# One run of small matmuls per step, from chunk 4 on, in an mLSTM and MLP kernel

## The chip, the cores and the metric

The kernel runs on one core of a Trainium2 chip. The metric is the device time of one execution in microseconds (us), as the median of several runs. The core's engines work side by side: PE (TensorE, matmuls; its weight loads are shown apart as PEld), DVE (VectorE), ACT (ScalarE), POOL (GpSimd) and SP, which here only issues transfers.

## What is computed

An mLSTM layer (4 batches, 8 heads, 768 tokens, head width 40) whose output goes through an MLP (320 to 2048 to 320):

```python
for t in range(S):
    m_new = np.maximum(f_gate[:, :, t] + m, i_gate[:, :, t])
    f_stab = np.exp(f_gate[:, :, t] + m - m_new)
    i_stab = np.exp(i_gate[:, :, t] - m_new)
    m = m_new
    C = f_stab[:, :, None, None] * C + i_stab[:, :, None, None] * np.einsum('bhd,bhe->bhde', vt, kt)
    n = f_stab[:, :, None] * n + i_stab[:, :, None] * kt
    h_tilde = np.einsum('bhde,bhe->bhd', C, qt)
    nq = np.einsum('bhd,bhd->bh', n, qt)[:, :, None]
    denom = np.maximum(np.abs(nq), 1.0)
    o = 1.0 / (1.0 + np.exp(-o_gate[:, :, t]))
    y[:, :, t] = o * h_tilde / denom
...
x = np.ascontiguousarray(attn_out.transpose(0, 2, 1, 3)).reshape(B * S, H * D)
...
h = x @ w_in
sp = np.maximum(h, 0.0) + np.log1p(np.exp(-np.abs(h)))
g = h * erf(sp)
return (g @ w_out).astype(np.float32)
```

## The kernel before

The 768 tokens are cut into 12 chunks of 64. A **step** is one chunk `c` for one pair of batches `r` (0 or 1), so there are 24 steps, two per chunk. A step has four groups of small matmuls, 16 each, on parts of the array of at most 64 rows and 64 columns; a trace shows each as two records, so a group counts 32:

- *carry* (L519): the queries scaled by the decay, `qe`, times the state that the earlier chunks left;
- *gain* (L524): keys times the weighted values `vg`, what this chunk adds to the state;
- *scores* (L510): keys times queries inside the chunk;
- *heads* (L532 from chunk 3 on, L537 before): the weights `dm` times the values. `dm` is the product of the scores and the decay factors, which DVE makes (L568).

`before(r)` holds carry and gain. From chunk 3 on (`JOIN = 3`) carry, gain and scores are one run of instructions on PE. From chunk 4 on three 128x128 transposes of the step of the chunk before (`turned`, L390) stand ahead of them in the same run. The heads are a run of their own, later, once DVE has made `dm`. Behind the heads DVE makes the denominator (`den`, L599 to L601), divides (L611, L613), gates (L618, L620) and brings the state up to date (L625, L628). The gated result is transposed by PE in the next chunk; ACT and DVE cut it into a high and a low part `xh` and `xl` (L403, L407), and these feed the MLP.

The MLP runs in 48 groups, 4 per chunk: up (L760, four products `h` of five matmuls each from group 16 on), a copy and an add to `hb` (ACT L771, DVE L776), softplus and erf on ACT (L780, L784; each change between them, or to exp, loads a table, L887), a product on DVE (L788), a split (L798 or L800, L804), and down (L828, L829, L826), whose results are copied out by L834 and L840.

PSUM holds six pieces that rotate or stay: `pa` has two slots of two banks each, `h` two of one bank, and two banks hold the MLP's results (`pob`). A step takes **both** `pa` slots: one tile `S` for the scores and the transposes, one tile `ph` for the sums `y` (carry plus heads) and `z` (gain).

The order is not left to a scheduler. `ORDER` lists the numbers of all operations in the sequence in which they are issued; a planner made it, with a cost in us for each operation (0.5 for the heads, 1.96 for the run with the transposes, and so on). Each engine works through its operations in that sequence and waits where an input or a slot is not ready.

Of the kernel before, what the change touches and what calls it, by code (L numbers as in the profile page):

```python
# [17 lines left out]
L = 64  # L18
# [15 lines left out]
class Plan:  # L34
# [137 lines left out]
def tile_mlstm_moe(  # L172
# [244 lines left out]
    def attention(c, prev=None):  # L417
# [93 lines left out]

        def before(r):
            y, z = pv(r), pk(r)
            st = state[r]
            for p in range(NPR if c else 0):
                for d in range(2):
                    for j in range(2):
# [431 lines left out]
```

## Time and profile before

| | |
|---|---|
| median of three runs | 454.5 us (454.19 to 454.68) |
| the profiled execution | 454.01 us, its span 452.3 us |
| PE busy | 439.0 us, 97% of the span |
| DVE, ACT, POOL busy | 79%, 75%, 9% |
| granted PE clock | 0.998 of full speed on average |

The profile is one execution. The span runs from the first instruction to the last, and the 1.7 us around it belong to the time but are not resolved. PE's matmuls overlap: a row shows how long one takes from start to end, while the distance between the starts of two neighbours is what the second costs the engine. So the timelines of PE are read by starts.

### The profile page before, as it was taken

What the parts mean: (1) busy time and instruction counts of PE and PEld (TensorE: products, weight loads), DVE (VectorE), ACT (ScalarE), POOL (GpSimd) and SP (SyncE); (2) the same over time, 40 slices, a digit from 0 to 9 for tenths busy, and PEclk for the clock granted to TensorE, in tenths of its full rate; (3) what the DMA queues carried; (4) which work ended last, traced back from release to release, by engine and by line L of the source; (5) the groups of instructions that cost most, each with busy time, mean ns of one, the idle gap of its engine ahead of it and who ended that gap; (6) DMA issues with size and microseconds to landing.
All of it is one profiled execution on the core that took longest, in us unless ns stands there. A gap on an engine that the chain in (4) does not pass through costs nothing.

```text
span 452.3 us, 13080 instructions
## 1 busy us (share of the span) xinstructions
PE 439.0 (97%) x5550; PEld 396.0 (88%) x5550; DVE 355.3 (79%) x710; ACT 338.5 (75%) x532; POOL 38.7 (9%) x62
## 2 busy tenths in 40 slices
PE   6979999999999999999999999999999999999996
PEld 3558988898999999989999998898998999999996
DVE  5899998799878887788969769878798856777471
ACT  4767999898767778978789796758996577783740
POOL 2000051004200102201300030000300000000000
PEclk9999999999999999999999999999999999999999
DMA  7989596847633144413315306132331000001011
GB/s 239 296 246 351 161 333 193 213 114 202 192 95 72 40 141 109 129 58 117 111 51 156 106 20 174 48 109 86 112 120 27 17 16 0 17 0 30 15 30 29
DMA packets 46826, 51.74 MB, mean 114 GB/s; under 512 B 27056, under 2 KB 31664, under 8 KB 46768
## 3 DMA queue, kind: packets, MB, share of 16 engines
q1 hardware_dynamic: 46768, 50.91, 38.6%
q8 instruction: 43, 0.70, 0.6%
q14 instruction: 15, 0.12, 0.1%
HBM read 46.77 MB, written 4.13 MB: 113 GB/s over the span
## 4 chain that ended last, share of the span: by engine, by line
PE 88%; DVE 7%; DMA 2%; issue 1%; ACT 1%; SPq 0%; DVEq 0%; ACTq 0%
PE h L760 39%; PE pob L828 12%; PE pob L826 11%; PE pob L829 11%; PE pa L519 3%; PE pa L532 2%; PE pa L510 2%; PE pob L824 2%; DMA raw<-in_w_in_dram 2%; PE pa L390 2%; PE pa L524 1%; DVE wo L725 1%; PE pa L826 1%; PE pa L829 1%; DMA gt<-in_gates_dram 1%
## 5 line engine op out<-in xcount | busy, mean ns | idle before, releaser
L760 PE MATMUL h<-xh,wh 128*128 128x256 f32 (+1 forms) x768 | 202.1, 343 | 1.0 <-DVE xh L407 0.6
L760 PEld LDWEIGHTS h<-xh,wh 128*128 128x128 f32 x768 | 125.7, 188 | 15.1 <-DVE xh L407 0.8
L760 PE MATMUL h<-xh,wl 128*128 128x256 f32 x384 | 107.9, 281 | 1.0 <-DVE wl L661 1.0
L771 ACT ACTIVATE hb<-h 128x256 f32<-128x256 f32 (+1 forms) x160 | 66.6, 421 | 55.9 <-PE h L760 55.4
L828 PE MATMUL pob<-woh,gh 128*128 128x320 f32 x336 | 101.5, 314 | 0.0
L829 PE MATMUL pob<-wo,gh 128*128 128x320 f32 x336 | 99.9, 309 | 0.0
L776 DVE TENSOR_TENSOR hb<-h,hb 128x256 f32<-128x256 f32 x128 | 53.4, 422 | 44.6 <-ACT hb L771 43.8
L887 ACT ACT_TABLE_LOAD x61 | 78.3, 1283 | 1.9 <-PEq L937 0.8
L760 PEld LDWEIGHTS h<-xh,wl 128*128 128x128 f32 x384 | 72.4, 188 | 2.9 <-DVE wl L661 1.2
L788 DVE TENSOR_TENSOR n<-n,hb 128x1024 f32<-128x1024 f32 x48 | 58.2, 1218 | 9.8 <-ACT n L784 9.8
L829 PEld LDWEIGHTS pob<-wo,gh 128*128 128x128 f32 x336 | 63.1, 188 | 1.7
L828 PEld LDWEIGHTS pob<-woh,gh 128*128 128x128 f32 x336 | 63.2, 188 | 0.9
L826 PE MATMUL pob<-woh,gl 128*128 128x320 f32 x336 | 61.6, 310 | 0.0
L488 POOL TENSOR_SCALAR_AFFINE_SELECT dm<-dm 128x512 f32<-128x512 f32 (+1 forms) x40 | 35.3, 888 | 286.1 <-ACT dm L468 220.0
L804 DVE TENSOR_TENSOR gl<-n,gh 128x1024 fp32r<-128x1024 f32 x45 | 55.4, 1232 | 0.2
L826 PEld LDWEIGHTS pob<-woh,gl 128*128 128x128 f32 x336 | 53.6, 188 | 1.8
L780 ACT ACTIVATE n<-hb 128x1024 f32<-128x1024 f32 x48 | 49.9, 1057 | 1.4 <-DVE hb L776 1.1
L784 ACT ACTIVATE n<-n 128x1024 f32<-128x1024 f32 x48 | 49.9, 1056 | 0.3
L798 ACT ACTIVATE gh<-n 128x1024 fp32r<-128x1024 f32 x29 | 30.3, 1055 | 2.3 <-DVE n L788 2.3
L834 ACT ACTIVATE o<-pob 128x320 f32<-128x320 f32 x22 | 9.6, 435 | 19.9 <-PE pob L826 19.7
L628 DVE TENSOR_TENSOR state<-state,pa 40x328 f32<-40x328 f32 (+1 forms) x36 | 17.8, 494 | 7.4 <-PE pa L532 5.9
L568 DVE TENSOR_TENSOR dm<-pa,dm 128x512 f32<-128x512 f32 x24 | 16.5, 686 | 4.2 <-PE pa L510 3.9
(103 smaller groups left out, 479.6 us busy)
## 6 DMA issues: line engine op xcount, KB each, us to landing
qk<-in_qk_dram SPq DMA_DIRECT2D x24, 512.0 KB
kvo<-in_kvo_dram SPq DMA_DIRECT2D x24, 484.0 KB
eT<-gd SPq DMA_DIRECT2D x44, 128.0 KB
raw<-in_w_out_dram SPq DMA_DIRECT2D x16, 320.0 KB
dm<-gd SPq DMA_DIRECT2D x40, 128.0 KB
raw<-in_w_in_dram SPq DMA_DIRECT2D x8, 512.0 KB
out_dram<-o SPq DMA_DIRECT2D x48, 80.0 KB
raw<-in_w_in_dram SPq DMA_DIRECT2D x4, 256.0 KB
```

What stands on the lines that cost most here:

```text
L488: nc.gpsimd.affine_select(out=x, in_=x, pattern=[[0, H], [1, L]], compare_op=ALU.is_ge, fill=0.0, base=base, channel_multiplier=-1)
L760: nc.tensor.matmul(h[:, n * T:n * T + n_], w, m, start=(s == 0), stop=(s == len(ops) - 1))
L771: nc.scalar.activation(part(), G(f'h{i}')[:, T:2 * T] if wide else G(f'h{i}'), AF.Copy)
L776: nc.vector.tensor_tensor(part(), G(f'h{i}')[:, 0:T], part(), op=ALU.add)
L780: nc.scalar.activation(new('n0', [128, 1024], ('n0', g)), G('hb'), AF.Softplus)
L784: nc.scalar.activation(G('n0'), G('n0'), AF.Erf)
L788: nc.vector.tensor_tensor(G('n0'), G('n0'), G('hb'), op=ALU.mult)
L804: nc.vector.tensor_tensor(new('gl', [128, 1024], ('gl', g), F32R), G('n0'), G('gh').bitcast(F32), op=ALU.subtract)
L826: nc.tensor.matmul(acc(b), G('gl')[:, ts], woh[:, j], start=False, stop=(j == NFF - 1))
L828: nc.tensor.matmul(acc(b), G('gh')[:, ts], woh[:, j], start=(j == 0), stop=False)
L829: nc.tensor.matmul(acc(b), G('gh')[:, ts], t['wol', j], start=False, stop=False)
L887: plan.run(ORDER, lambda k: nc.scalar.preload_act_table_set(KIND[k]), stay)
```

## The change

From chunk 4 on (`LATE = 4`) a step has one PSUM tile, `S`, and one run of small matmuls. The run of step (c, r) is: its own carry and scores, then the heads and the gain of the step that came before it, (c, 0) for (c, 1) and (c-1, 1) for (c, 0). The first run, of step (4, 0), has carry and scores alone, and the heads of the very last step, (11, 1), stay a run of their own (`rest`). So the heads and the gain come half a chunk later than the scores, and the denominator, the division, the gating and the state's update of a step move behind the next step's run.

In the tile, `y` lies behind the scores in its bank, and `z` is written over the scores, which DVE has read by then. The banks of `z` are also dealt out otherwise (`d ^ j` in place of `d`). The three transposes become an operation of their own, `turn`, and write into the same tile once `y` and `z` have been read; the six of chunk 3 are done at once (`turn_both`). All matmuls of the program stay, in number and shape. `ORDER` is made anew from about the 100th us of the program on; the operations before that keep their places on PE.

```diff
-PLAIN, JOIN, GH_ACT, WIDE_UP = (0, 1, 2), 3, 32, 16
+PLAIN, JOIN, LATE, GH_ACT, WIDE_UP = (0, 1, 2), 3, 4, 32, 16
...
+        joint, late = c >= JOIN, c >= LATE
+        home = 'S' if late else 'ph'
...
+        aty, atz = (256, 0) if late else (0, NPR * V1)
+        pv = lambda r, c=c: side(A(home, r, c))[:, :, aty:aty + NPR * V1].rearrange("p j (n d) -> p j n d", d=V1)
+        pk = lambda r, c=c: side(A(home, r, c))[:, :, atz:atz + NPR * V1].rearrange("p d (n e) -> p d n e", e=V1)
...
-                        nc.tensor.matmul(x[sides[d], j, p * L:(p + 1) * L], k, q, start=True, stop=True)
-
-        def before(r):
+                        nc.tensor.matmul(x[sides[d], j, p * L:(p + 1) * L], k, q, start=not late, stop=True, skip_group_check=late)
+
+        def carry(r):
...
+        def gain(r, c=c):
+            z = pk(r, c)
+            for p in range(0 if c == NC - 1 else NPR):
                 for j in range(2):
                     for d, ds in enumerate(sides):
                         h, n = 2 * p + j, D if j or joint else 64
-                        nc.tensor.matmul(z[64 * j:64 * j + n, d, p], A('kvo', r)[ds, h * D:h * D + n], A('vg', r)[ds, h],
-                                         start=(c == 0 and p == 0), stop=False)
...
+                        nc.tensor.matmul(z[64 * j:64 * j + n, d ^ j if late else d, p], A('kvo', r, c)[ds, h * D:h * D + n],
+                                         A('vg', r, c)[ds, h], start=(late or c == 0) and p == 0, stop=late, skip_group_check=late)
...
+        def turn(r, c):
+            plan.part = f'a{c}{r}'
+
+            @op('PE', 0.42, mm=3, r=turned_from(c, r) + [K('S', r, 'y', c)] + ([] if c == NC - 1 else [('st', r)]),
+                w=[K('S', r, 'p', c)], kind='m', tile_=[('xh', ('xh', c)), ('xl', ('xl', c))] * (r == 0))
+            def _():
+                if r == 0:
+                    room(c)
+                turned(c, r, t['S', c, r][:, 0:3 * W])
...
+            step = ((c, 0) if r else (c - 1, 1)) if late and (r or c > LATE) else ()
...
-                if joint:
+                if joint and not late:
                     new('pa', [128, 1024], ('ph', c, r))
                 if was:
                     turned(*was, A('S', r)[:, 256:256 + 3 * W])
                 if joint:
-                    before(r)
+                    carry(r)
+                    if not late:
+                        gain(r)
                 scores(r)
+                if step:
+                    heads(step[1], step[0])
+                    gain(step[1], step[0])
...
+                if step:
+                    after(step[1], step[0])
+                    turn(step[1], step[0])
```

What the new order looks like on the engines is seen best at single steps. PE before, at the run of a step of chunk 6 (`pa` tiles carry numbers here: 2835 is `S`, 2836 is `ph`; `L390` is the step of the chunk before, its result `kvo` transposed):

```order
L829 MATMUL pob0_76<-wo_1758,gh_2438 128x320
L390 MATMUL pa_2835<-ident_65,kvo_1890 128x128 x3
L519 MATMUL pa_2836<-state0_71,qe_2782 64x41 x16
L524 MATMUL pa_2836<-vg_2694,kvo_1744 40x41 x16
L510 MATMUL pa_2835<-qk_2700 64x64 x16
L760 MATMUL h_2892<-xh_2048,wh_73 128x512
```

PE before, at the separate heads of a step of chunk 4:

```order
L829 MATMUL pob0_76<-wo_1817,gh_1931 128x320
L532 MATMUL pa_1983<-kvo_1858,dm_1559 64x41 x16
L826 MATMUL pob0_76<-woh_75,gl_1955 128x320 x4
L828 MATMUL pob0_76<-woh_75,gh_1953 128x320
L829 MATMUL pob0_76<-wo_1742,gh_1953 128x320
```

The first piece has carry, gain and scores behind the transposes; the second is a run of 16 small matmuls between large ones.

PE of the changed kernel, at a run of chunk 6 (2736 is the tile of the step itself, 2483 that of the step before; L520, L512, L537 and L529 are carry, scores, heads and gain, and L831, L899 and L900 are up and down):

```order
L900 MATMUL pob0_76<-wo_1875,gh_2410 128x320
L520 MATMUL pa_2736<-state0_71,qe_2645 64x41 x16
L512 MATMUL pa_2736<-qk_2609 64x64 x16
L537 MATMUL pa_2483<-kvo_1764,dm_1580 64x41 x16
L529 MATMUL pa_2483<-vg_2661,kvo_1764 40x41 x16
L831 MATMUL h_2803<-xh_2243,wh_73 128x512
```

All four groups now stand in one row, and two tiles of two steps are written in it.

ACT of the changed kernel, where the first `xh` of chunk 4 is made from the transposes (L403), and what stands right ahead of it and behind it (L869 is the copy `gh`, L842 the copy `hb`, L958 a table load):

```order
L855 ACTIVATE n0_2025<-n0_2025 128x1024
L958 ACT_TABLE_LOAD
L470 ACTIVATE dm_1927<-dm_1927 128x512
L869 ACTIVATE gh_2251<-n0_1970 128x1024
L842 ACTIVATE hb_2147<-h_2218 128x512
L403 ACTIVATE xh_2243<-pa_1977 128x3x128
L958 ACT_TABLE_LOAD
```

The tile 1977 is free for the next run only when this `xh` and the `xl` behind it on DVE are done. ACT has 58 table loads in the changed kernel, 61 before.

## Rows read from the trace of the kernel before

**Rows 1.** The page's head and first part: busy us, share of the span, instructions.
```profile
span 452.3 us, 13080 instructions
PE 439.0 (97%) x5550; PEld 396.0 (88%) x5550; DVE 355.3 (79%) x710; ACT 338.5 (75%) x532; POOL 38.7 (9%) x62
PEclk9999999999999999999999999999999999999999
```

**Rows 2.** Stretches: each engine's busy us (instructions), granted clock, DMA share, GB/s.
```profile
core 0: us, PE busy (x) PEld busy (x) DVE busy (x) ACT busy (x) POOL busy (x), PEclk, DMA share, GB/s
100.00:125.00 25.00, 24.38 (x271) 22.24 (x270) 23.28 (x49) 20.64 (x34) 8.01 (x8) 1.00 0.65 186
...
125.00:390.00 265.00, 265.00 (x3305) 242.31 (x3304) 210.17 (x424) 205.31 (x311) 19.89 (x24) 1.00 0.28 82
390.00:448.30 58.30, 58.27 (x373) 55.61 (x371) 36.70 (x50) 31.45 (x45) 0.00 (x0) 1.00 0.09 20
```

**Rows 3.** PE's timeline at a step of chunk 4: start us, us, instruction, count.
```profile
119.58 0.41 PE L760 MATMUL h<-xh,wh 128*128 128x256 f32 x2
119.83 0.49 PE L390 MATMUL pa<-ident,kvo 128*128 128x128 f32 x3
120.25 0.68 PE L519 MATMUL pa<-state,qe 40*64 40x41 f32 x32
120.73 0.50 PE L524 MATMUL pa<-vg,kvo 64*40 64x41 f32 x32
121.05 0.68 PE L510 MATMUL pa<-qk 40*64 40x64 f32 x32
121.65 0.41 PE L828 MATMUL pob<-woh,gh 128*128 128x320 f32 x1
121.90 0.31 PE L829 MATMUL pob<-wo,gh 128*128 128x320 f32 x1
122.05 0.31 PE L828 MATMUL pob<-woh,gh 128*128 128x320 f32 x1
...
122.79 0.31 PE L829 MATMUL pob<-wo,gh 128*128 128x320 f32 x1
123.03 0.68 PE L532 MATMUL pa<-kvo,dm 64*64 64x41 f32 x32
123.63 0.85 PE L826 MATMUL pob<-woh,gl 128*128 128x320 f32 x4
124.33 0.31 PE L828 MATMUL pob<-woh,gh 128*128 128x320 f32 x1
```

**Rows 4.** PE's timeline at three transposes that stand alone, near the end.
```profile
377.51 0.40 PE L760 MATMUL h<-xh,wh 128*128 128x512 f32 x1
377.75 0.49 PE L390 MATMUL pa<-ident,kvo 128*128 128x128 f32 x3
377.99 0.39 PE L828 MATMUL pob<-woh,gh 128*128 128x320 f32 x1
378.23 0.31 PE L829 MATMUL pob<-wo,gh 128*128 128x320 f32 x1
378.37 0.31 PE L828 MATMUL pob<-woh,gh 128*128 128x320 f32 x1
```

**Rows 5.** PE's weight loads by shape, 125 to 390 us: busy us, mean ns, idle before.
```profile
L510 PEld LDWEIGHTS pa<-qk 40*64 40x64 f32 x480 | 8.6, 134 | 0.0
L519 PEld LDWEIGHTS pa<-state,qe 40*64 40x64 f32 x480 | 8.4, 134 | 2.5 <-issue 2.0 <-DVE hb L776 0.3 <-DVE dm L464 0.2
L532 PEld LDWEIGHTS pa<-kvo,dm 64*64 64x64 f32 x480 | 8.4, 134 | 3.2 <-issue 2.7 <-DVE hb L776 0.2
L524 PEld LDWEIGHTS pa<-vg,kvo 64*40 64x40 f32 x416 | 5.3, 114 | 0.0
```

**Rows 6.** PE's timeline where it waits for split weights, about 104 and 108 us.
```profile
103.60 0.55 PE L828 MATMUL pa<-woh,gh 128*128 128x320 f32 x1
103.99 0.31 PE L829 MATMUL pa<-wo,gh 128*128 128x320 f32 x1
...
107.36 0.30 PE L828 MATMUL pa<-woh,gh 128*128 128x320 f32 x1
108.28 0.42 PE L829 MATMUL pa<-wo,gh 128*128 128x320 f32 x1 [0.62 <-DVE wo L725]
```

**Rows 7.** DVE's timeline behind a step's heads (which start on PE at 187.91).
```profile
188.66 1.00 DVE L628 TENSOR_TENSOR state<-state,pa 40x328 f32<-40x328 f32 x2 [0.64 <-PE pa L532]
...
190.37 0.17 DVE L599 TENSOR_SCALAR den<-pa 128x8 f32<-128x8 f32 x1
...
191.35 0.66 DVE L613 TENSOR_TENSOR kvo<-pa,den 64x160 f32<-64x160 f32 x2
```

**Rows 8.** PE's timeline at the run that follows them.
```profile
191.55 0.75 PE L826 MATMUL pob<-woh,gl 128*128 128x320 f32 x4
192.15 0.49 PE L390 MATMUL pa<-ident,kvo 128*128 128x128 f32 x3
```

**Rows 9.** ACT's and DVE's timelines behind the lone transposes of 377.75 us.
```profile
378.35 1.28 ACT L887 ACT_TABLE_LOAD   x1
379.64 1.06 ACT L784 ACTIVATE n<-n 128x1024 f32<-128x1024 f32 x1
380.61 0.47 ACT L403 ACTIVATE xh<-pa 128x384 fp32r<-128x384 f32 x1
...
381.11 0.56 DVE L407 TENSOR_TENSOR xh<-pa,xh 128x384 fp32r<-128x384 f32 x1 [1.19 <-ACT xh L403]
```

More of the change, by code (lines that the diff above doesn't have):

```diff
@@ L499, in _ @@
                                             A('dm', r)[:, :, L - 1:L].to_broadcast([128, H, V1]), op=ALU.mult)
-        ends = lambda x: x.rearrange("p (i w) -> p i w", i=4)[:, 0:4:3]
+        ends = lambda x: side(x)[:, :, 0:256] if late else x.rearrange("p (i w) -> p i w", i=4)[:, 0:4:3]
         def scores(r):
@@ L509, in scores @@
                         q, k = (A('qk', r)[js, d, i, p] for i in range(2))
-                        nc.tensor.matmul(x[sides[d], j, p * L:(p + 1) * L], k, q, start=True, stop=True)
-        def before(r):
-            y, z = pv(r), pk(r)
-            st = state[r]
+                        nc.tensor.matmul(x[sides[d], j, p * L:(p + 1) * L], k, q, start=not late, stop=True, skip_group_check=late)
+        def carry(r):
+            y, st = pv(r), state[r]
             for p in range(NPR if c else 0):
@@ L518, in before @@
                         js = slice(64 * j, 64 * j + D)
-                        nc.tensor.matmul(y[lies(d, j), j, p], A('qe', r)[js, d, p], st[js, d, p], start=(p == 0), stop=False)
-            for p in range(0 if last else NPR):
+                        nc.tensor.matmul(y[lies(d, j), j, p], A('qe', r)[js, d, p], st[js, d, p], start=(p == 0), stop=False,
+                                         skip_group_check=late)
+        def gain(r, c=c):
+            z = pk(r, c)
+            for p in range(0 if c == NC - 1 else NPR):
                 for j in range(2):
@@ L531, in heads @@
                     for d, ds in enumerate(sides):
-                        nc.tensor.matmul(y[lies(d, j), j, p], w[ds, j, p], v[ds, 2 * p + j], start=False, stop=(p == NPR - 1))
+                        nc.tensor.matmul(y[lies(d, j), j, p], w[ds, j, p], v[ds, 2 * p + j], start=False, stop=(p == NPR - 1),
+                                         skip_group_check=late)
             for p in range(0 if joint else NPR):
@@ L537, in heads, with weigh @@
                         nc.tensor.matmul(y[os, j, p], w[ds, j, p, ts], v[ds, 2 * p + j], start=False, stop=(p == NPR - 1))
-        early = dict(r=lambda r: ([('st', r), K('qe', r)] if c else []) + ([] if last else [K('vg', r), K('kvo', r, 'k')]),
-                     cost=(0.49 if c else 0) + (0 if last else 0.41), mm=(32 if c else 0) + (0 if last else 32))
+        def weigh(r):
+            plan.part = f'a{c}{r}'
+            @op('DVE', 0.6, r=[K('S', r)], w=[K('dm', r)])
+            def _():
+                x = ends(A('S', r)).rearrange("p j (n t) -> p j n t", t=L)
+                nc.vector.tensor_tensor(dm(r), x, dm(r), op=ALU.mult)
@@ new lines, in after, with _ @@
+        def after(r, c=c):
+            plan.part = f'a{c}{r}'
+            st = state[r]
+            ph = K(home, r, 'y' if late else 0, c)
+            if c == 0:
+                @op('ACT', 0.34, r=[ph], w=[('st', r)])
+                def _():
+                    nc.scalar.activation(st[0:CR], pk(r)[0:CR], AF.Copy)
+            @op('DVE', 0.52, r=[ph], w=[K('den', r, 0, c)], tile_=('den', ('den', c, r)))
+            def _():
+                den = new('den', [128, 2, NPR], ('den', c, r))
+                nq = pv(r, c)[:, :, :, D]
+                nc.vector.tensor_scalar(out=den, in0=nq, scalar1=1.0, scalar2=2.0, op0=ALU.max, op1=ALU.mult)
+                nc.vector.scalar_tensor_tensor(out=den, in0=nq, scalar=-2.0, in1=den, op0=ALU.mult, op1=ALU.max)
+                nc.vector.reciprocal(den, den)
+            by_head = lambda x: x.rearrange("p (n j d) -> p j n d", j=2, d=D)
+            @op('DVE', 0.75 if joint else 0.41, r=[ph, K('den', r, 0, c)], w=[K('kvo', r, 'k', c)])
+            def _():
+                y, z, den = by_head(A('kvo', r, c)[:, 0:DM]), pv(r, c)[:, :, :, 0:D], A('den', r, c).unsqueeze(3)
+                if not joint:
+                    nc.vector.tensor_tensor(y, z, den.to_broadcast([128, 2, NPR, D]), op=ALU.mult)
+                    return
+                nc.vector.tensor_tensor(y[:, 0], z[:, 0], den[:, 0].to_broadcast([128, NPR, D]), op=ALU.mult)
+                for to, at in (sides, sides[::-1]):
+                    nc.vector.tensor_tensor(y[to, 1], z[at, 1], den[at, 1].to_broadcast([64, NPR, D]), op=ALU.mult)
+            @op('DVE', 0.63 if c >= JOIN else 0.43, r=[K('kvo', r, 'k', c)], w=[K('kvo', r, 'o', c)])
+            def _():
+                y = th(r, c)
+                nc.vector.scalar_tensor_tensor(out=y, in0=y, scalar=1.0, in1=A('kvo', r, c)[:, 0:DM], op0=ALU.add, op1=ALU.mult)
+                if c >= JOIN:
+                    nc.vector.tensor_copy(A('kvo', r, c)[:, KV + 320:KV + 384], A('kvo', r, c)[:, KV + 256:KV + 320])
+            if c != NC - 1 and c > 0:
+                @op('DVE', 1.3 if joint else 0.93, r=[K('eT', r, 0, c), ph], w=[('st', r)])
+                def _():
+                    nc.vector.tensor_tensor(st[0:CR], st[0:CR], A('eT', r, c)[0:CR, :, :, L - 1:L].to_broadcast([CR, 2, NPR, V1]),
+                                            op=ALU.mult)
+                    for rows in (slice(0, D), slice(64, CR)) if joint else (slice(0, CR),):
+                        z = pk(r, c)[rows]
+                        nc.vector.tensor_tensor(st[rows], st[rows], z[:, ::-1] if late and rows.start else z, op=ALU.add)
@@ new lines, in turn, with _, turn_both @@
+        def turn(r, c):
+            plan.part = f'a{c}{r}'
+            @op('PE', 0.42, mm=3, r=turned_from(c, r) + [K('S', r, 'y', c)] + ([] if c == NC - 1 else [('st', r)]),
+                w=[K('S', r, 'p', c)], kind='m', tile_=[('xh', ('xh', c)), ('xl', ('xl', c))] * (r == 0))
+            def _():
+                if r == 0:
+                    room(c)
+                turned(c, r, t['S', c, r][:, 0:3 * W])
+        def turn_both(c):
+            plan.part = f'a{c}1'
+            @op('PE', 0.84, mm=6, r=turned_from(c, 0) + turned_from(c, 1), w=[(('p', c), 0)], kind='m', tile_=('pa', ('p', c)))
+            def _():
+                p = new('pa', [128, 1024], ('p', c))
+                for n in range(2):
+                    turned(c, n, p[:, 512 * n:512 * n + 3 * W])
@@ L541, in attention, with room @@
+        def room(c):
+            x = new('xh', [128, 3, 2, T], ('xh', c), F32R)
+            for i, n in enumerate(('xh', 'xl')):
+                t[n, c] = x[:, :, i]
+            t['x', 'both', c] = x
+        early = dict(r=lambda r: ([('st', r), K('qe', r)] if c else []) + ([] if last or late else [K('vg', r), K('kvo', r, 'k')]),
+                     cost=(0.49 if c else 0) + (0 if last or late else 0.41), mm=(32 if c else 0) + (0 if last or late else 32))
         for r in range(2):
             plan.part = f'a{c}{r}'
-            was = (prev, r) if prev is not None else ()
@@ L545, in _ @@
-            @op('PE', 0.64 + (0.42 if was else 0) + (early['cost'] if joint else 0),
-                r=[K('qk', r, n) for n in 'qk'] + ([] if c else [('warm', 0)]) + turned_from(*was) + (early['r'](r) if joint else []),
-                w=[K('S', r)] + ([K('ph', r, 'k')] if joint else []) + ([K('S', r, 'p')] if was else []),
-                tile_=[('pa', ('S', c, r))] + ([('pa', ('ph', c, r))] if joint else []), kind='a',
-                mm=32 + (3 if was else 0) + (early['mm'] if joint else 0), after=[K('dm', r)])
@@ L550, in _ @@
-            def _(r=r, was=was):
+            was = (prev, r) if prev is not None and not late else ()
+            step = ((c, 0) if r else (c - 1, 1)) if late and (r or c > LATE) else ()
+            reads, writes, mm, cost = [], [], 0, 0
+            if step:
+                k, n = step
+                reads = [K('dm', n, 0, k), K('kvo', n, 'v', k)] + ([] if k == NC - 1 else [K('vg', n, 0, k), K('kvo', n, 'k', k)])
+                writes, mm, cost = [K('S', n, 'y', k)], 32 + 32 * (k < NC - 1), 0.5 + 0.41 * (k < NC - 1)
@@ new lines, in _ @@
+            @op('PE', 0.64 + cost + (0.42 if was else 0) + (early['cost'] if joint else 0),
+                r=[K('qk', r, n) for n in 'qk'] + ([] if c else [('warm', 0)]) + turned_from(*was) + (early['r'](r) if joint else []) + reads,
+                w=[K('S', r)] + ([K('ph', r, 'k')] if joint and not late else []) + ([K('S', r, 'p')] if was else []) + writes,
+                tile_=[('pa', ('S', c, r))] + ([('pa', ('ph', c, r))] if joint and not late else []), kind='a',
+                mm=32 + mm + (3 if was else 0) + (early['mm'] if joint else 0), after=[K('dm', r)])
@@ L551, in _ @@
+            def _(r=r, was=was, step=step):
                 new('pa', [128, 1024], ('S', c, r))
-                if joint:
+                if joint and not late:
                     new('pa', [128, 1024], ('ph', c, r))
@@ L556, in _, with rest @@
                 if joint:
-                    before(r)
+                    carry(r)
+                    if not late:
+                        gain(r)
                 scores(r)
+                if step:
+                    heads(step[1], step[0])
+                    gain(step[1], step[0])
+            if late:
+                weigh(r)
+                if step:
+                    after(step[1], step[0])
+                    turn(step[1], step[0])
+                if r == 0:
+                    if c == LATE:
+                        turn_both(prev)
+                    divided(prev, [K('S', n, 'p', prev) if c > LATE else (('p', prev), 0) for n in range(2)])
+        if late:
+            def rest():
+                plan.part = f'a{c}1'
+                @op('PE', 0.5, mm=32, r=[K('dm', 1), K('kvo', 1, 'v')], w=[K('S', 1, 'y')], kind='a')
+                def _():
+                    heads(1)
+                after(1)
+                turn(1, c)
+                divided(c, [K('S', n, 'p') for n in range(2)])
+            return rest
         if prev is not None:
@@ L563, in attention @@
         for r in range(2):
-            plan.part = f'a{c}{r}'
-            @op('DVE', 0.6, r=[K('S', r)], w=[K('dm', r)])
-            def _(r=r):
-                s = ends(A('S', r)).rearrange("p j (n t) -> p j n t", t=L)
-                nc.vector.tensor_tensor(dm(r), s, dm(r), op=ALU.mult)
+            weigh(r)
         for r in range(2):
@@ L578, in _ @@
                     new('pa', [128, 1024], ('ph', c, r))
-                    before(r)
+                    carry(r)
+                    gain(r)
                 if r == 0:
-                    x = new('xh', [128, 3, 2, T], ('xh', c), F32R)
-                    for i, n in enumerate(('xh', 'xl')):
-                        t[n, c] = x[:, :, i]
-                    t['x', 'both', c] = x
+                    room(c)
                 heads(r)
         for r in range(2):
-            plan.part = f'a{c}{r}'
@@ L589, in attention @@
-            st = state[r]
-            if c == 0:
-                @op('ACT', 0.34, r=[K('ph', r)], w=[('st', r)])
-                def _(r=r, st=st):
-                    nc.scalar.activation(st[0:CR], pk(r)[0:CR], AF.Copy)
-            @op('DVE', 0.52, r=[K('ph', r)], w=[K('den', r)], tile_=('den', ('den', c, r)))
-            def _(r=r):
-                den = new('den', [128, 2, NPR], ('den', c, r))
-                nq = pv(r)[:, :, :, D]
-                nc.vector.tensor_scalar(out=den, in0=nq, scalar1=1.0, scalar2=2.0, op0=ALU.max, op1=ALU.mult)
-                nc.vector.scalar_tensor_tensor(out=den, in0=nq, scalar=-2.0, in1=den, op0=ALU.mult, op1=ALU.max)
-                nc.vector.reciprocal(den, den)
@@ L603, in attention @@
-            by_head = lambda x: x.rearrange("p (n j d) -> p j n d", j=2, d=D)
-            @op('DVE', 0.75 if joint else 0.41, r=[K('ph', r), K('den', r)], w=[K('kvo', r, 'k')])
-            def _(r=r):
-                y, z, den = by_head(A('kvo', r)[:, 0:DM]), pv(r)[:, :, :, 0:D], A('den', r).unsqueeze(3)
-                if not joint:
-                    nc.vector.tensor_tensor(y, z, den.to_broadcast([128, 2, NPR, D]), op=ALU.mult)
-                    return
-                nc.vector.tensor_tensor(y[:, 0], z[:, 0], den[:, 0].to_broadcast([128, NPR, D]), op=ALU.mult)
-                for to, at in (sides, sides[::-1]):
-                    nc.vector.tensor_tensor(y[to, 1], z[at, 1], den[at, 1].to_broadcast([64, NPR, D]), op=ALU.mult)
@@ L615, in _ @@
-            @op('DVE', 0.63 if c >= JOIN else 0.43, r=[K('kvo', r, 'k')], w=[K('kvo', r, 'o')])
-            def _(r=r):
-                y = th(r)
-                nc.vector.scalar_tensor_tensor(out=y, in0=y, scalar=1.0, in1=A('kvo', r)[:, 0:DM], op0=ALU.add, op1=ALU.mult)
-                if c >= JOIN:
-                    nc.vector.tensor_copy(A('kvo', r)[:, KV + 320:KV + 384], A('kvo', r)[:, KV + 256:KV + 320])
-            if not last and c > 0:
-                @op('DVE', 1.3 if joint else 0.93, r=[K('eT', r), K('ph', r)], w=[('st', r)])
-                def _(r=r, st=st):
-                    nc.vector.tensor_tensor(st[0:CR], st[0:CR], A('eT', r)[0:CR, :, :, L - 1:L].to_broadcast([CR, 2, NPR, V1]),
-                                            op=ALU.mult)
-                    for rows in (slice(0, D), slice(64, CR)) if joint else (slice(0, CR),):
-                        nc.vector.tensor_tensor(st[rows], st[rows], pk(r)[rows], op=ALU.add)
+            after(r)
@@ L845, in tile_mlstm_moe @@
             gate_block(k)
-        attention(k, prev)
+        rest = attention(k, prev)
         if prev is not None:
@@ L873, in tile_mlstm_moe @@
     if prev is not None:
-        finish(prev)
+        rest()
         for g in range(4 * prev, 4 * prev + 4):
```

17 lines of the change are left out of this document (7 added, 10 removed), and 122 rows, old and new, of the table ORDER.

## The prediction

> **What bounds the kernel now.** I read the page's first part, then the busy times by stretch, then PE's timeline. PE is busy 97% of the span [rows 1]; the reader should look at the stretches behind that mean. From 125 to 390 us PE is busy 265.00 of 265.00 us, and from there to 448.3 us all but 0.03 us; DVE and ACT are busy about 79% and 77% in the long stretch, and the clock is 1.00, the upper level of 2.4 GHz, all the time [rows 2]. So no wait ends last there: the time is the sum of what PE's instructions cost, and only fewer or cheaper instructions, or less lost between them, shorten it. Between 100 and 125 us PE loses a little, and DVE, at 23.28 of 25 us, is nearly as full [rows 2].
>
> PE's timeline then shows what is lost between instructions; it is to be read by starts. Inside a row of large matmuls the next L828 or L829 starts 0.15 us after the last (121.90 to 122.05) [rows 3]. At the border of a run of small ones this spacing breaks three times. **Into** the run: L829 at 122.79, the heads at 123.03, so 0.24, 0.09 too much. **Out** of it: the heads take 0.60 to the next large start, while 32 small ones with the same weight loads (carry, 120.25 to 120.73) take 0.48 when another small group follows: 0.12 more. **Behind** it: 121.65 to 121.90 is 0.25, 0.10 too much, and the four L826 from 123.63 to 124.33 take 0.70 in place of 4 x 0.147, 0.11 too much [rows 3]. A border pair thus costs 0.09 + 0.12 + 0.10 = 0.31 us.
>
> **The change, part by part.** Matmuls and their shapes stay; the runs of small ones fall from 46 in the program to 31, counted in the two orders. The 15 that go are heads: of the 16 steps from chunk 4 on, all but the last give up their own run.
>
> *A step before* [rows 3]: from the transposes at 119.83 to the large matmul at 121.65 is 1.82, plus 0.10 behind, 1.92. Its heads: 0.09 in, 0.60, 0.11 behind, 0.80. Together 2.72 us.
>
> *A step after.* The run: in 0.09; carry 0.48; scores 0.48 to 0.50 (their 0.60 less the way out, 0.11); heads 0.48; gain 0.32 (120.73 to 121.05) plus the way out, 0.45; behind it 0.10. That is 2.10. The transposes now stand alone; their price is shown near the end: 377.75 to 377.99 is 0.24, and the next large start comes 0.24 later in place of 0.15, so 0.33 [rows 4]. In the old run they cost 0.42 (119.83 to 120.25) [rows 3], of which 0.09 is the way in that the new run pays itself, so moving them costs nothing. Together 2.43 us.
>
> The difference is 0.29 a step, and 15 x 0.29 = **4.4 us**, all of it on PE and so on the path that sets the end.
>
> *What isn't shown.* Scores followed by heads, and heads followed by gain, occur nowhere before. Between groups that do follow each other the hand-over is at most 0.04 us (carry's 0.48 to gain against 31 spacings). It could be dearer, since the heads' first matmuls wait for DVE, POOL and transfers. The ends are 0.02 and 0.31 (a full border); I take 0.04, since carry to gain also waits for DVE and a transfer and costs just that. A gain from a dearer hand-over is excluded.
>
> *The late heads.* The denominator, division, gating and state update stay on DVE in number and size (I take the reversed bank order in the state's add as free; both banks are read anyway), and come half a chunk later. Who waits for them: the next run needs the state, and a run's tile is free again only when `xh` and `xl` have read the transposes. Before, the tight place was another: both slots belonged to one step, and the next run waited for DVE to read `ph`. At 188.66 DVE begins with the state, the last division ends at 192.01 [rows 7], and the next run enters at 192.15, without a gap behind the four L826 [rows 8]: 0.1 us to spare. After, state and division have until the transposes and the run after, 5 us and more of PE work. The new tight place is transposes to next run. By the order, five of these distances are short: three times four L826 and ten wide (or sixteen narrow) L831, 2.46 us, then 3.05 and 3.64; the others are over 5 us. `xh` takes 0.47 and `xl` 0.56, together 1.1 us with the hand-over [rows 9]. So 1.4 us are to spare if ACT and DVE come at once; the cover is PE's up and down matmuls.
>
> *ACT* loses three table loads of 1.28 us [rows 9]; off the path, nothing.
>
> *The reshuffled stretch, 100 to 125 us.* PE waits there for DVE's split weights: 0.39 between 103.60 and 103.99 and 0.92 between 107.36 and 108.28, in place of 0.15 each, so 1.0 us [rows 6]. The new order lets sixteen up matmuls ahead of the first of them and spreads the splits, which could save all of it; but DVE has no more room than before. Between 1.0 saved and 2 lost (the longer wait, 0.8, twice, and a bit) I take 0.3 saved, near the present state.
>
> **Sum.** Profiled execution 454.0 - 4.4 - 0.3 = 449.3 us. The median of the runs stands 0.5 above the profiled one, so **449.8 us**.
>
> **The rivals.**
>
> *The hand-over is a border too.* If PE drains between scores and heads because the heads' inputs are waited for there, 0.27 of the 0.29 a step is given back: the change then doesn't do what it says: 15 x 0.27 = 4.1, 453.9. Half of it gives 451.8. For it speaks that an entry shows up to 0.2 us idle of the weight loads ahead of heads under "issue" (2.7 us in 15 heads) [rows 5]; against it that carry to gain and gain to scores, with waits, show nothing of the kind.
>
> *Banks.* Before, gain's two row halves write two banks; with `d ^ j` neighbours of different row halves write one bank. Heads do that already, and need 0.48 to a follower just as carry does, whose row halves write different banks; so the rows give this no price. Gain's lower price goes with its narrower weights, 114 against 134 ns a load [rows 5]. If it were the banks after all, gain would cost what heads cost: 0.16 more in 14 steps, 2.2 us, 452.0. The Trainium skill, "TensorEngine Tiling (Array Packing)", Restrictions and Gotchas, says that different row tiles cannot access the same PSUM bank at once; by that rule 452.0, and the trace of the heads speaks against a price.
>
> *Late `xh`: slower.* ACT works in order. At 377.75 the transposes stand alone, and `xh` begins only at 380.61, behind a table load and an erf; `xl` ends at 381.67, 3.7 us after the transposes' end [rows 4, 9]. Before, no run waited for that. With this delay at all five short places PE would wait 3 x 1.2 + 0.7, 4.3 us: 454.1, no change. One more 1024-wide pass of 1.06 ahead of `xh` makes it 3 x 2.3 + 1.7 + 1.1, 9.7 us: 459.5. It ends slower from a mean wait of 1.2 us at the five places on. Against it: at the places I followed, the order has `hb`, `gh` or `dm`, not a table load, right ahead of `xh`; at one of the five a load stands two places ahead.
>
> *Scattered waits*, 1 to 3 us in all, most likely about 100 to 125 us: 451 to 452.5.
>
> **How the numbers follow.** Forecast 0.66; scattered waits 0.12; dear hand-over 0.08 (half of it within 0.2%); banks 0.05; late `xh` 0.09 (slower, or no change at its edge). The range, 448.2 to 453.2, goes from all of the early waits saved and a cheap hand-over to the rivals that keep a small gain; it leaves the last rival and the full border out, with some of the forecast's own edge. A run can tell 0.2%, 0.9 us, from no change. Faster 0.87, same 0.06, slower 0.07.
>
> **What would show it.** In the changed profile L520, L512, L537 and L529 should follow each other in about 2.0 us, 15 times less a border; L390 alone should show 0.24 and 0.24 again; PE should be as full from 125 us on. The prediction is wrong if heads start more than 0.55 us behind the start of the scores, if gain takes 0.45, or if PE's timeline shows gaps before L520 that end with DVE `xh` L407.

## The result and the profile after

The changed kernel takes **451.09 us** (median of 6 runs, 450.6 to 452.0), the kernel before beside it 454.83: a ratio of 0.991, 95% interval 0.988 to 0.994. So it is faster, as forecast, but by less: 3.7 us (0.9%) in place of 4.7. The time lies inside the range that was given. Its page, to be read against [rows 1]:

```profile
span 450.0 us, 13070 instructions
PE 436.6 (97%) x5550; PEld 395.6 (88%) x5550; DVE 356.8 (79%) x710; ACT 332.7 (74%) x529; POOL 41.1 (9%) x62
```

PE has the same 5550 instructions and lost 2.4 us of busy time; ACT lost three instructions, the table loads. The windows of time, as in [rows 2] (busy us of each engine, granted clock, DMA share, GB/s):

```profile
100.00:125.00 25.00, 23.61 (x234) 20.96 (x233) 24.58 (x47) 22.11 (x38) 4.73 (x6) 1.00 0.62 176
125.00:390.00 265.00, 264.79 (x3390) 244.73 (x3389) 213.07 (x429) 198.47 (x309) 25.52 (x26) 1.00 0.30 86
390.00:446.00 56.00, 55.95 (x359) 53.48 (x357) 35.13 (x47) 32.02 (x45) 0.00 (x0) 1.00 0.07 17
```

From 125 us on PE is as full as before and the clock is at its upper level. Between 100 and 125 us PE idles 1.4 us where it had idled 0.6, and DVE is busy 24.58 of 25. PE's timeline at a run of chunk 5, and at lone transposes (start us, us, instruction, count), answers [rows 3, 4]:

```profile
137.98 0.49 PE L390 MATMUL pa<-ident,kvo 128*128 128x128 f32 x3
138.23 0.83 PE L897 MATMUL pob<-woh,gl 128*128 128x320 f32 x4
...
140.58 0.40 PE L831 MATMUL h<-xh,wh 128*128 128x256 f32 x2
140.91 0.68 PE L520 MATMUL pa<-state,qe 40*64 40x41 f32 x32
141.40 0.67 PE L512 MATMUL pa<-qk 40*64 40x64 f32 x32
141.89 0.63 PE L537 MATMUL pa<-kvo,dm 64*64 64x41 f32 x32
142.33 0.50 PE L529 MATMUL pa<-vg,kvo 64*40 64x41 f32 x32
142.76 0.51 PE L831 MATMUL h<-xh,wh 128*128 128x256 f32 x2
143.11 0.28 PE L831 MATMUL h<-xh,wl 128*128 128x256 f32 x1
```

Here `h<-xh` is up, `woh,gl` is down, and L520, L512, L537 and L529 are carry, scores, heads and gain. The second L831 of the pair at 140.58 starts 0.12 later, so the way in takes 0.21 in place of the usual 0.12: 0.09 too much. Scores follow carry after 0.49, heads follow scores after 0.49, gain follows heads after 0.44: no border inside. The whole run takes 1.85 to the next large start, and the two L831 behind it take 0.35 in place of 0.24. The other runs of the changed kernel that hold all four groups show the same 1.85, but for one of 1.92 at 287.4 us.

**A ruler without the first 100 us.** Up to a row of L895 at about 100 us (L824 in the kernel before) PE's order is the same in both kernels, yet this row starts between 98.8 and 102.8 us in the nine profiled executions of this study. So a single execution carries up to 4 us of chance ahead of the change; in this one PE waited 2.6 us for DVE's `xh` at about 30 us, in the profile of before 0.6. From there the distance to the last four matmuls that read `gl` is steadier: the changed kernel's two executions give 344.73 and 344.62. Before, and after:

```profile
99.43 1.34 PE L824 MATMUL pa<-wo,n 128*128 128x320 f32 x4
...
447.52 0.75 PE L826 MATMUL pob<-woh,gl 128*128 128x320 f32 x4
```

```profile
100.47 1.34 PE L895 MATMUL pa<-wo,n 128*128 128x320 f32 x4
...
445.20 0.75 PE L897 MATMUL pob<-woh,gl 128*128 128x320 f32 x4
```

That is 348.09 and 344.73 us, 3.4 us less; the profiled spans differ by 2.3 only because this execution of the changed kernel came 1.0 late to the first row. I use this distance, called the ruler, beside the medians.

| kernel | median us | ruler: from, to | us |
|---|---|---|---|
| before | 454.8 | 99.43, 447.52 | 348.09 |
| changed | 451.1 | 100.47, 445.20 | 344.73 |
| changed, again (e_after) | 451.8 | 101.13, 445.75 | 344.62 |
| one border a run (e_border) | 458.3 | 102.78, 453.67 | 350.89 |
| same matmul ahead (e_ahead) | 452.4 | 100.51, 447.42 | 346.91 |
| three borders a run (e_three) | 467.2 | 99.06, 460.24 | 361.18 |
| DVE order (e_dve) | 448.8 | 98.82, 441.57 | 342.75 |
| no masks (e_nomask) | 449.8 | 102.70, 444.55 | 341.85 |
| xh three times (e_xh) | 458.0 | 101.01, 452.12 | 351.11 |

**Where the rest went.** PE's waits between 112 and 120 us, with POOL and DVE beside them (the bracket is idle time and who ended it). POOL runs the masks here, affine selects that zero the decay weights of later tokens (L490). On DVE, L585 and L587 gate, L796 splits the down weights, L859 makes the product, and L875 splits it into `gl`:

```profile
111.05 4.93 POOL L490 TENSOR_SCALAR_AFFINE_SELECT dm<-dm 128x512 f32<-128x512 f32 x6 [34.79 <-ACT dm L470]
...
111.34 0.94 DVE L585 SCALAR_TENSOR_TENSOR kvo<-kvo 128x320 f32<-128x320 f32 x1
...
112.31 0.56 DVE L587 COPY kvo<-kvo 128x64 f32<-128x64 f32 x1
...
112.78 2.69 DVE L796 TENSOR_TENSOR wo<-wo,woh 128x320 fp32r<-128x320 f32 x3
112.92 0.14 PEld L390 LDWEIGHTS pa<-ident,kvo 128*128 128x128 f32 x1 [0.36 <-DVE kvo L587]
...
114.67 0.41 PE L900 MATMUL pa<-wo,gh 128*128 128x320 f32 x1
...
115.39 1.66 DVE L859 TENSOR_TENSOR n<-n,hb 128x1024 f32<-128x1024 f32 x1
115.52 0.19 PEld L900 LDWEIGHTS pa<-wo,gh 128*128 128x128 f32 x1 [0.55 <-DVE wo L796]
...
118.36 1.22 DVE L875 TENSOR_TENSOR gl<-n,gh 128x1024 fp32r<-128x1024 f32 x1
...
119.63 1.44 PE L897 MATMUL pa<-woh,gl 128*128 128x320 f32 x8 [0.75 <-DVE gl L875]
```

By starts, against the usual spacing, PE loses 0.28 ahead of the last transposes, 0.26 and 0.46 ahead of two L900 and 0.91 ahead of L897. With 0.24 at 106.9, 0.20 at 121.2, 0.23 at 147.7 and 0.29 at 260.3 that is 2.9 us; the kernel before loses 0.24 and 0.78 [rows 6] and two smaller ones, 1.3 in all. The 0.24 in either sum is no wait for DVE: the profile shows no idle time of PE or its weight loads there, and the second L899 or L900 behind a row of L895 (L824 before) comes that late in all nine traces. It stands on both sides and drops out. So 1.6 us came back, nearly all of it as waits for DVE, and the work itself fell by 3.4 + 1.6 = 5.0 us. Behind a wait the next matmul starts about 0.1 late as well (114.67 to 114.92 is 0.25 in place of 0.15); with that, both figures are about 0.2 larger.

### The profile page after: what moved, and what is told of

Same layout as the page of the kernel before. It is cut to its first block, busy times and chain, and to the rows that moved or that the text cites. A ratio compares the mean times of both kernels' runs of the same rounds, so it can differ in the third digit from the quotient of the medians.

```text
span 450.0 us, 13070 instructions
## 1 busy us (share of the span) xinstructions
PE 436.6 (97%) x5550; PEld 395.6 (88%) x5550; DVE 356.8 (79%) x710; ACT 332.7 (74%) x529; POOL 41.1 (9%) x62
## 4 chain that ended last, share of the span: by engine, by line
PE 86%; ACT 4%; DVE 4%; DMA 3%; issue 1%; POOL 0%; SPq 0%; DVEq 0%; POOLq 0%
PE h L831 37%; PE pob L899 11%; PE pob L900 11%; PE pob L897 11%; PE pa L520 3%; PE pa L512 2%; PE pob L895 2%; PE pa L537 2%; DMA raw<-in_w_in_dram 1%; PE pa L529 1%; PE pa L390 1%; ACT L958 1%; DMA dm<-gd 1%; PE pob L284 1%; PE pa L449 1%
## 5 line engine op out<-in xcount | busy, mean ns | idle before, releaser
L831 PE MATMUL h<-xh,wh 128*128 128x256 f32 (+1 forms) x768 | 206.4, 346 | 2.7 <-DVE xh L407 2.6
L831 PEld LDWEIGHTS h<-xh,wh 128*128 128x128 f32 x768 | 128.1, 190 | 16.6 <-DVE xh L407 2.8
L842 ACT ACTIVATE hb<-h 128x256 f32<-128x256 f32 (+1 forms) x160 | 66.3, 421 | 72.8 <-PE h L831 72.5
L831 PE MATMUL h<-xh,wl 128*128 128x256 f32 x384 | 108.4, 282 | 0.2 <-DVE wl L732 0.2
L899 PE MATMUL pob<-woh,gh 128*128 128x320 f32 x336 | 100.8, 312 | 0.0
L900 PE MATMUL pob<-wo,gh 128*128 128x320 f32 x336 | 99.9, 309 | 0.0
L831 PEld LDWEIGHTS h<-xh,wl 128*128 128x128 f32 x384 | 72.9, 190 | 1.6 <-DVE wl L732 0.4
L859 DVE TENSOR_TENSOR n<-n,hb 128x1024 f32<-128x1024 f32 x48 | 58.8, 1229 | 9.0 <-ACT n L855 8.9
L900 PEld LDWEIGHTS pob<-wo,gh 128*128 128x128 f32 x336 | 63.1, 188 | 1.6
L899 PEld LDWEIGHTS pob<-woh,gh 128*128 128x128 f32 x336 | 63.3, 188 | 0.2
L490 POOL TENSOR_SCALAR_AFFINE_SELECT dm<-dm 128x512 f32<-128x512 f32 (+1 forms) x40 | 37.7, 951 | 277.9 <-ACT dm L470 274.5
L897 PE MATMUL pob<-woh,gl 128*128 128x320 f32 x336 | 62.5, 310 | 0.0
L897 PEld LDWEIGHTS pob<-woh,gl 128*128 128x128 f32 x336 | 54.4, 188 | 2.3
L875 DVE TENSOR_TENSOR gl<-n,gh 128x1024 fp32r<-128x1024 f32 x45 | 54.8, 1227 | 0.3
L869 ACT ACTIVATE gh<-n 128x1024 fp32r<-128x1024 f32 x29 | 30.5, 1056 | 0.0
```

The costliest lines, as they stand in the source:

```text
L490: nc.gpsimd.affine_select(out=x, in_=x, pattern=[[0, H], [1, L]], compare_op=ALU.is_ge, fill=0.0, base=base, channel_multiplier=-1)
L831: nc.tensor.matmul(h[:, n * T:n * T + n_], w, m, start=(s == 0), stop=(s == len(ops) - 1))
L842: nc.scalar.activation(part(), G(f'h{i}')[:, T:2 * T] if wide else G(f'h{i}'), AF.Copy)
L859: nc.vector.tensor_tensor(G('n0'), G('n0'), G('hb'), op=ALU.mult)
L875: nc.vector.tensor_tensor(new('gl', [128, 1024], ('gl', g), F32R), G('n0'), G('gh').bitcast(F32), op=ALU.subtract)
L897: nc.tensor.matmul(acc(b), G('gl')[:, ts], woh[:, j], start=False, stop=(j == NFF - 1))
```

## Experiments

### Is the gain the borders?

e_border puts one matmul into the run of the changed kernel, between scores and heads: a full 128 x 128 weight load, 64 columns, into columns that nobody reads. In e_ahead the same call stands ahead of `carry(r)`. Line numbers of the kernel shift by a few where lines are added:

```diff
+        def wide_one(r):
+            nc.tensor.matmul(A('S', r)[:, 420:484], wh[:, 0, 0:128], wh[:, 0, 128:192], start=False, stop=True, skip_group_check=True)
...
                 scores(r)
                 if step:
+                    wide_one(r)
                     heads(step[1], step[0])
```

> The changed kernel again, unchanged, as the measure for the other runs of this group. Expected 451.1 us. The profiled execution read so far had PE waiting 2.6 us for DVE xh L407 at 29 to 35 us, in a part where both kernels have the same order. If this is the transfers of one execution, another execution shows another figure there (0.6 to 1.6 as in the kernel before), and the waits of PE for DVE between 112 and 120 us (0.28, 0.26, 0.46 and 0.91 us) come back, since they follow from DVE's order; if those are chance too, they are gone or stand elsewhere.

> One matmul of 128 x 64 with a full 128 x 128 weight load, into columns that nobody reads, between the scores and the heads in each of the 15 runs of the changed kernel: the old border comes back and nothing else is moved. Theory (the gain is the borders): 15 times the matmul's own cost (an estimate from 0.12 to 0.14 us a start beside large ones: 2 us) and 15 x 0.27 to 0.32 = 4.1 to 4.9 us of borders, so about 457.2 (456.8 to 458.2). Rival (the gain came from the changed order on DVE and ACT, three table loads and later heads, and a border costs nothing): 453.2, the own cost alone.

> The same 15 matmuls of 128 x 64, but ahead of the carry, next to the large matmuls, so that no border is added. Both theories: 451.1 and 15 times the own cost of 0.12 to 0.14 us, 453.1 (452.6 to 453.5). What tells the theories apart is the difference between the run with the matmul inside and this one: 4.1 to 4.9 us by the border theory, under 0.5 us by the rival.

e_after came to 451.8 us with the same four waits (0.29, 0.25, 0.46, 0.91), so these follow from the order; its early waits were others. e_border came to 458.3 and e_ahead to 452.4: a difference of 5.9 us, by the ruler 4.0. PE's timeline at the same run, first e_border, then e_ahead:

```profile
143.17 0.40 PE L835 MATMUL h<-xh,wh 128*128 128x256 f32 x2
143.50 0.68 PE L523 MATMUL pa<-state,qe 40*64 40x41 f32 x32
143.99 0.67 PE L515 MATMUL pa<-qk 40*64 40x64 f32 x32
144.59 0.30 PE L506 MATMUL pa<-wh 128*128 128x64 f32 x1
144.82 0.68 PE L540 MATMUL pa<-kvo,dm 64*64 64x41 f32 x32
145.31 0.50 PE L532 MATMUL pa<-vg,kvo 64*40 64x41 f32 x32
```

```profile
140.63 0.40 PE L836 MATMUL h<-xh,wh 128*128 128x256 f32 x2
140.87 0.20 PE L506 MATMUL pa<-wh 128*128 128x64 f32 x1
141.00 0.68 PE L523 MATMUL pa<-state,qe 40*64 40x41 f32 x32
141.49 0.67 PE L515 MATMUL pa<-qk 40*64 40x64 f32 x32
```

With the matmul inside, scores to matmul is 0.60, matmul to heads 0.23, heads to gain 0.49: 1.32 in place of 0.49 + 0.44, 0.39 more. Ahead of carry it makes the entry 0.25 in place of 0.21, 0.04 more: its own cost nearly vanishes in the way in that is there anyway, where I had expected 0.12. So a border, priced as the same matmul inside the run against ahead of it, is 0.35 us, and 15 of them are 5.2 us. All 15 runs of e_border show the same 0.34 up to the heads. By the ruler the two differ by less, since each execution has waits of its own. e_ahead has three (0.61 at 182, 0.65 at 184 and 0.52 at 323 us); without them it is 0.5 us longer than e_after, 15 x 0.03. e_border has one of 0.92 at 328 us; without all these the difference is 4.8 us. The rival that the gain came from other changes of the order is out: everything else was left as it was, and the borders alone give back the 5.0 us that the work had lost.

> The narrow-column matmul of the run with one border put not only between scores and heads, but also between carry and scores and between heads and gain: 15 + 15 + 14 of them. The run with one border spent 0.386 us a run more than the changed kernel by its trace (scores to the matmul 0.604, from it to the heads 0.227, heads to gain 0.488, against 0.494 and 0.439). Theory (any switch to a full-size matmul and back costs that, whatever the groups): 44 x 0.386 = 17.0 us over the changed kernel in the part of the trace behind 100 us, a median of 468 us (466 to 470). Rival (the border is dear only ahead of the heads, whose inputs come from DVE, POOL and transfers): 15 x 0.386 + 29 x 0.034 (the matmul's own cost beside large ones) = 6.8 us, 458.

e_three, with the call also between carry and scores and between heads and gain, measured 467.2; by the ruler it is 16.5 us longer than the changed kernel, 44 x 0.375 (0.5 of it is a wait of its own at 330 us). The four groups of a run now start at:

```profile
140.62 0.68 PE L523 MATMUL pa<-state,qe 40*64 40x41 f32 x32
...
141.45 0.69 PE L515 MATMUL pa<-qk 40*64 40x64 f32 x32
...
142.31 0.68 PE L540 MATMUL pa<-kvo,dm 64*64 64x41 f32 x32
...
143.14 0.52 PE L532 MATMUL pa<-vg,kvo 64*40 64x41 f32 x32
```

That is 0.83, 0.86 and 0.83 in place of 0.49, 0.49 and 0.44, so 0.34, 0.37 and 0.39 more. The border is no matter of the heads and their inputs; it costs about the same at all three places.

### Is the give-back DVE's order?

> The changed kernel with five DVE operations moved in the order: the weight splits 12 and 15 (L796) behind the gating of chunk 3 (L585, L587) and the splits 10 and 11; L859 of group 10 and the splits 1 and 2 (L796) behind the second vg (L500) of chunk 4. PE's, POOL's and the transfers' orders stay. Theory (the give-back of 1.6 us is DVE's order between 112 and 120 us): the waits of 0.28, 0.26, 0.46 and 0.91 us go and no others come, so 1.3 to 2.0 us less than the changed kernel in the same group, 449.4. Rival (DVE as a whole is full there, slowed by POOL's masks, and any order only moves the wait): within 0.5 us of the changed kernel, with the same sum of waits at other instructions between 112 and 140 us.

Five numbers of the order table, all of them work of DVE, moved: 273 and 279 behind 271, and 435, 251 and 253 behind 522. **448.8 us** (448.1 to 450.4), 0.987 of the kernel before (0.983 to 0.990): faster than both kernels, and by the ruler 1.9 to 2.0 us shorter than the changed one's two executions. Its DVE and PE about 110 us, and its window from 100 to 125 us:

```profile
108.65 0.48 DVE L585 SCALAR_TENSOR_TENSOR kvo<-kvo 128x320 f32<-128x320 f32 x1
109.17 0.20 DVE L587 COPY kvo<-kvo 128x64 f32<-128x64 f32 x1
109.28 3.95 DVE L796 TENSOR_TENSOR wo<-wo,woh 128x320 fp32r<-128x320 f32 x5
...
110.45 0.82 PE L390 MATMUL pa<-ident,kvo 128*128 128x128 f32 x6
...
113.73 1.21 DVE L875 TENSOR_TENSOR gl<-n,gh 128x1024 fp32r<-128x1024 f32 x1
```

```profile
100.00:125.00 25.00, 24.44 (x226) 23.17 (x225) 23.45 (x45) 23.79 (x37) 5.85 (x6) 1.00 0.60 168
```

The six transposes run through in 0.82 in place of 1.16 us, `gl` begins 14.9 us behind the first row of the ruler in place of 17.9, and the four waits are gone; 0.44 come back ahead of L520, for DVE's `xh`. PE's order is the same instruction for instruction and most of what was lost there is won, so the rival (DVE full, any order only moves the wait) is out. The masks still lengthen the splits here (five L796 take 3.95 us), but PE no longer waits for these.

### Does POOL slow DVE?

e_nomask leaves the masks out from chunk 4 on, and with them a part of the computation:

```diff
-                    for rows, base in ((128, L), (64, 0)):
+                    for rows, base in () if c >= LATE else ((128, L), (64, 0)):
```

> The changed kernel without POOL's masks (affine selects on the decay weights, L490) from chunk 4 on, so that later tokens enter the sum: part of the computation is left out, and nothing is moved. In the changed kernel DVE's instructions are longer while POOL runs from 111.05 to 115.98: L585 0.94 in place of 0.49, L587 0.56 in place of 0.20, three L796 2.69 in place of 1.5, L859 1.66 in place of 1.22, 2.4 us together, and PE's waits of 0.28, 0.26, 0.46 and 0.91 us for DVE stand right there and behind. Theory (POOL's masks slow DVE, and with DVE's order that makes the waits): DVE's instructions fall back to the shorter figures, PE's waits of 1.9 us between 112 and 120 go, and so do the 0.23 at 147.8 and the 0.29 at 260.3: 1.9 to 2.4 us less behind 100 us than the changed kernel, a median near 449.2. Rival (DVE's longer records have another cause, transfers into the same memory for example): the durations and the waits stay, 451.4.

449.8 us, and by the ruler 2.8 to 2.9 us shorter than the changed kernel's two executions. DVE's timeline at the same instructions:

```profile
113.57 0.49 DVE L585 SCALAR_TENSOR_TENSOR kvo<-kvo 128x320 f32<-128x320 f32 x1
114.10 0.20 DVE L587 COPY kvo<-kvo 128x64 f32<-128x64 f32 x1
114.20 1.54 DVE L796 TENSOR_TENSOR wo<-wo,woh 128x320 fp32r<-128x320 f32 x3
115.66 1.22 DVE L859 TENSOR_TENSOR n<-n,hb 128x1024 f32<-128x1024 f32 x1
```

0.94, 0.56, 2.69 and 1.66 fell to 0.49, 0.20, 1.54 and 1.22, and all of PE's waits between 112 and 120 us are gone, those at 147.7 and 260.3 too; ahead of L520 the wait grew by 0.17, for `xh`. The rival with another cause of the long records (transfers) is out: the masks alone were taken away. So two things made the give-back, each shown by its own run: DVE's order, and POOL's masks that lie beside it.

### What late `xh` costs

e_xh makes ACT's copy three times:

```diff
-                nc.scalar.activation(t['xh', c][:, :, ts], pt(), AF.Copy)
+                for _ in range(3 if c >= LATE else 1):
+                    nc.scalar.activation(t['xh', c][:, :, ts], pt(), AF.Copy)
```

> The changed kernel with ACT's copy of the transposes (xh, L403, 0.49 us) made three times instead of once from chunk 4 on: xh and xl come 0.98 us later, everything else stays. It prices the rival that late xh stops the next run. The prediction reckoned 1.4 us to spare at the five short places; then no run waits and the time stays 451.4 (within 0.5). By the changed kernel's trace xl ended 0.14 us ahead of the run at 183.5, 0.83 ahead of that at 336.3, 0.94 at 269.6, 1.16 at 140.9 and 1.29 at 218.6, over 1.8 at the others: then waits of about 0.9, 0.2 and 0.1 us come ahead of L520, 1.2 us, and ACT's 30 us of further work may add as much again elsewhere: 452.6 to 454.

458.0 us, by the ruler 6.4 us longer than the changed kernel: far over both figures. ACT, DVE and PE behind the transposes of 182.16 us:

```profile
182.89 1.53 ACT L404 ACTIVATE xh<-pa 128x384 fp32r<-128x384 f32 x3
...
183.69 0.50 PE L832 MATMUL h<-xh,wh 128*128 128x512 f32 x1 [0.45 <-DVE hb L848]
...
186.21 0.68 PE L521 MATMUL pa<-state,qe 40*64 40x41 f32 x32 [0.39 <-DVE xh L408]
```

Ahead of the runs PE waits longer at three places (154.4, 186.2 and 274.0 us by 0.2, 0.4 and 0.8), about 1.5 us. The sum is near the 1.2 that was expected, the places are only in part: one wait ends with `xh`, the other two with `qe`, which DVE also makes. Most of the rest are waits of 0.1 to 0.9 ahead of L832 (up), for `hb`: ACT is busy 347 us in place of 333 (32 further copies of 0.47, 15 us, not the 30 that I had put down), and the reading of the up matmuls' result stands in the same queue. I had left those out. So the run prices more than late `xh`: it fills ACT's queue as well.

## Why the prediction came out as it did

- **What bounds the kernel** held: from 125 us on PE is full, and less work on PE shortened the time by as much, but for the waits.
- **The borders**: forecast 15 x 0.29 = 4.4, measured 5.0 to 5.2 as work, and 5.2 by putting them back. The joins are free, scores to heads and heads to gain as well as carry to scores. The heads inside the run took 0.44 to the next group in place of the 0.48 that I counted; behind a large matmul (e_border) they take 0.49. So the 0.48 of a group behind a large matmul seems to hold some of the border's cost; no run separates it.
- **The transposes alone**: moving them costs nothing, as forecast. They take 0.25, and some 0.08 more stand behind them (four L897 take 0.67 from 138.23 on, usually 0.59).
- **The reshuffled stretch** is the term that was mis-sized. I took 0.3 us saved, within bounds of 1.0 saved and 2 lost; 1.6 were lost, most of them in 100 to 125 us. I wrote that DVE has no more room than before, and then chose a value near no change. The row of DVE at 23.28 of 25 us [rows 2] spoke for the upper bound: the new order brought the gating of chunk 3, its splits and the next chunk's masks closer together, and POOL's masks lengthen just those instructions of DVE. The wait behind the 0.92 in [rows 6] looks like the same thing already: four L725 took 3.29 us there, from 105.46 on, beside masks that ran from 103.06 to 107.89, and seven of them 2.90 us from 100.19 on, beside none. I read it as order alone; no run took the masks out of the kernel before. The 0.39 of [rows 6] I read as a wait too, and it is none (see above); so at most 0.8 could have been saved.

```profile
100.19 2.90 DVE L725 TENSOR_TENSOR wo<-wo,woh 128x320 fp32r<-128x320 f32 x7
...
103.06 4.83 POOL L488 TENSOR_SCALAR_AFFINE_SELECT dm<-dm 128x512 f32<-128x512 f32 x4 [27.84 <-ACT dm L468]
...
105.46 3.29 DVE L725 TENSOR_TENSOR wo<-wo,woh 128x320 fp32r<-128x320 f32 x4
```

- **The median**: 454.5 - 5.0 + 1.6 = 451.1, the measured time; that it fits to a tenth is chance, since from the 454.83 measured beside it the sum is 451.4. By its number it is the case "scattered waits", 451 to 452.5, which I gave 0.12; the forecast's mechanism was right and one term mis-sized by 1.9 us, of which the borders gave 0.6 back.
- **Dear hand-over** is out: the joins show no border, and where one was put, 5.2 us came.
- **Banks** is out: gain takes 0.43 to the next large start, way out included, where 0.45 was reckoned without a price for the banks, and its weight loads take 116 ns in place of 114 [rows 5]. The Trainium skill, "TensorEngine Tiling (Array Packing)", Restrictions and Gotchas, says that different row tiles cannot access the same PSUM bank at once; these rows show no price of that.
- **Late `xh`** did not cost anything here, but by luck. At 183.5 us `xl` ended 0.14 us ahead of the run, where I had reckoned 1.4: DVE came to it 1 us after ACT was done. The run's weight loads already stood idle for it; PE, which entered after the usual 0.33, lost nothing. A disturbance finds that place (e_ahead, e_xh).

```profile
182.86 0.54 DVE L407 TENSOR_TENSOR xh<-pa,xh 128x384 fp32r<-128x384 f32 x1
183.54 0.56 PEld L520 LDWEIGHTS pa<-state,qe 40*64 40x64 f32 x32 [0.26 <-DVE xh L407]
```

- **The signs**: heads start 0.49 behind scores, under the 0.55 that was to be a sign of a border. The sign for gain, 0.45, is also what the forecast's own sum has for gain with the way out, so it can only be meant without it; gain took 0.43 with it. A gap of PE itself ahead of L520 that ends with `xh` does not stand in the profile. The nearest is the 0.20 at 121.2, which the profile puts down to PE's own L897 although `xl` ended 0.14 us ahead of it; in e_dve and e_nomask the wait at that place ends with `xh`.

Open stays what shifts the first 100 us by up to 4 us from one execution to the next. In the profile of the changed kernel ACT waits 2.0 us and DVE 1.7 us for a piece of the up weights to land, at 27 to 29 us, and the `xh` that PE waits for stands behind these in DVE's queue; the longest wait for a landing there in the profile of before is 0.5. That points to the transfers, but no run tested it.

## What to carry over

Where TensorE is full, count the changes between full-size and small tiled matmuls: each way there and back cost about 0.35 us here, at the three places tried, while small groups joined to each other cost nothing. A new order of a full engine's queue is worked out like any other term: walk the helper engine's queue up to each instruction that the full engine waits for, with the other engines that run beside it. To compare two executions, start at a row up to which both do the same.

## What was unexpected in the hardware

While POOL ran a mask (an affine select on 128 x 512), 13 of the 28 DVE instructions beside it whose operands all lie in SBUF (changed kernel, from 98 us on) took 0.3 to 0.5 us longer than usual: 0.49 to 0.94 (L585), 0.20 to 0.56 (L587), 1.22 to 1.66 (L859). Those that read PSUM did not: L407 took 0.54 to 0.56 beside masks in the changed kernel, and 0.55 beside none. Without masks the longer figures vanish. It goes both ways: a mask takes 0.65 us where DVE does nothing in SBUF alone, and 1.6 to 1.7 where L875 (1.21 us, not longer than usual) had begun just ahead of it, as at 258.6 and 297.6 us.

The Trainium skill, "SBUF — State Buffer", SBUF: two separate sides, describes an exclusive lock on a pair of ports that GpSimd shares with some of DVE's instructions: the one that starts first holds it for its whole instruction, and the other waits. These rows agree with it in kind, in both directions; that this lock is the cause is not shown by a run.
